# Outputs of one chunk in one run with the next chunk's state products and scores, five shared PSUM banks, and a new order of the first 42 tasks

## The chip, the cores and the metric

The kernel runs on one core of one Trainium2 chip. The metric is device time in microseconds; the median of three runs of the kernel before is 540.75 (540.54 to 540.91). A profile is one execution recorded instruction by instruction, in which PE is TensorE, PEld its weight loads, DVE VectorE, ACT ScalarE, POOL GpSimd and SP the engine that issues most of the transfers.

## The reference

Attention of the RWKV kind goes through 768 steps in 4 batches of 8 heads of 48 channels; its output, 3072 tokens of 384 channels, goes through a feed-forward layer of width 2048.

```python
for t in range(S):
    cur = np.einsum('bhd,bhe->bhde', u[None] * kt, vt)
    y[:, :, t] = np.einsum('bhd,bhde->bhe', rt, state + cur)
    state = wt[:, :, :, None] * state + np.einsum('bhd,bhe->bhde', kt, vt)
...
h = x @ w_in
g = h * (1.0 / (1.0 + np.exp(-1.702 * h)))
return g @ w_out
```

All tensors are float32; r, k, v and w vary per step, u per channel.

## The kernel before, in words

**Attention.** The tokens are cut into 24 chunks of 128 steps, six for each batch. Heads go in four pairs, so rows of a tile are channels (112, with 16 empty ones) and columns are pair and step. `chunk(t)` is a generator; each `next` on it is one piece, token `a<t>` in the order. Its steps: products of the decays from the end and from the start of the chunk (two scans, lines 239 and 245, into `lp`), keys and queries scaled by them (`kq`, 260 and 261), r times k (`rku`, 252), its sum with u (`ps_d`, 267, copied to `s`, 270), keys transposed (`ps_t`, 283, copied to `kt`, 285), the diagonal mask times s (`am`, 292), state updates (`ps_u`, 305) and scores (311) in two banks, the running states `mid` and `sf` (277, 316, 319), scores put over the mask (322), outputs (`ps_y`, 329) and what the states add to them in two halves (340). Between the halves a one-element operation on `mid` that reads the last output bank (349), called the guard here, keeps the second half behind the first. Then the output is split into a high and a low float32r part of `x` (205, 206). From chunk 8 on, s comes from VectorE alone (255, 272, 273).

**Feed-forward.** Four chunks make a group of 512 tokens. A task is one group and one of 16 blocks of the width; the first group's first tasks are cut into halves of 256 tokens, 20 half-width tasks, so there are 106. A task has a first product (token `g`, nine matmuls, 384 to 386, into `ph`), a gelu on ScalarE twice and a subtraction on VectorE (token `h`, 395 to 397, `gh`, `gf`, `gl`), and a second product (token `y`, nine matmuls, 410 to 412, into three banks `po`). Missing rows of `x` are filled by small transfers (token `x`, line 372).

**Weights.** They arrive in twelve pieces (token `f`) and are converted to a high and a low part in four steps each (token `w`, lines 191 to 201) on ScalarE and VectorE, during the first 110 us or so.

**Order.** Each engine does its instructions in the order in which the program issues them. Up to task 42 that order is the list of tokens in `RAMP`; from there `rest()` derives it from `PARTS`, which says for each piece of a chunk at which task before its group's start, and on which side of that task's products, it stands. Token `d` issues dummy matmuls on `warm` (365), `l` loads of a chunk (`wkr_t` in two buffers, on SP and POOL in turn; `v_t` in three), `m` a check of magnitudes on ScalarE (211). PSUM has eight banks: three `po`, two for `ph` and the dummies, three for all attention products.

Of the kernel before, what the change touches and what calls it, by code (L numbers as in the profile page):

```python
# [1 line left out]

# [9 lines left out]
I32 = mybir.dt.int32  # L12
# [35 lines left out]
WHOLE = 8  # L48
LAG = 2
# [15 lines left out]
l0 a0 l0 M a0 a0 d20 l0 l1 m0 a0 f0 a0 a0 d3 a1 a1 a0 a0 d12 a0 m0 a1 a0 a1 a0 l1 f1 a1 a1 d3 w0 l2 a1 m1 a1  # L65
d18 w0 a1 a2 a1 a2 a2 w1 w0 a1 d3 a2 a2 m1 a2 d4 w1 m2 a2 l3 l2 a3 f2 a3 m2 w1 x1 w0 a2 d12 a3 a3 w2 a2 f3 g0
w1 m3 l3 f4 a3 h0 g1 h1 a3 a2 y0 w3 y1 w2 w3 l4 a3 f5 a2 a3 a3 w2 m3 a3 w2 w3 a3 x3 g2 h2 w3 g3 h3 g4 y2 w4 a4
y3 f6 h4 w4 g5 w5 g6 h5 y4 w5 w4 g7 h6 w4 h7 a4 w5 y5 w5 g8 h8 w6 g9 y6 g10 y7 h9 y8 g11 f7 w6 w7 w7 h10 y9
g12 h11 w6 w6 g13 w7 l4 w7 h12 y10 h13 y11 g14 a4 f8 f9 w8 y13 g15 h14 y12 w9 l5 g16 w8 a4 h15 w9 w8 m4 w8 y14
y15 h16 g17 w9 a4 a4 g18 a5 h17 a5 f10 y16 h18 g19 g20 a5 a4 y17 w9 h19 w10 y18 w10 m4 f11 a4 l5 a5 a4 h20 l6  # L70
w11 w10 y19 l7 w11 g21 h21 m5 y20 g22 a5 w10 m5 a6 w11 a5 l6 a4 w11 a4 a5 g23 a6 a5 a5 y21 h22 a6 a6 m6 a5 a6
a7 l8 a5 a7 a6 y22 a6 a7 a6 m6 g24 a7 a6 l7 a7 h23 a7 a6 a6 a7 a7 a7 g25 l9 a7 h24 l8 a7 m7 a8 h25 y23 u a8 a8
x7 m7 y24 y25 l9 g26 m8 a8 h26 g27 h27 g28 a8 a8 y26 a8 y27 a9 a9 h28 g29 l10 y28 a8 g30 a9 m8 h29 a8 m9 g31
h30 a9 a9 l10 a9 a8 a10 a9 a8 y29 g32 y30 h31 y31 a10 a9 h32 l11 a9 g33 g34 l11 m9 a10 m10 h33 y32 g35 m10 a10
a10 a9 h34 a9 a10 l12 g36 a11 a11 y33 h35 a10 g37 a11 h36 y34 m11 h37 a10 a10 g38 a11 a11 g39 m11 a12 a10 l12
a12 a10 a12 a11 a12 a11 a12 y35 h38 y36 a11 l13 a11 a12 h39 g40 a11 m12 l13 a11 x11 y37 l14 m12 a12 y38 g41
y39 h40 a12 a13 h41 l14
# [6 lines left out]
def rwkv_ffn_kernel(ctx: ExitStack, tc, wkr, vp, vrk, ub, w_in, w_out, masks, vt, uc, out):  # L84
# [6 lines left out]
    ps_h = ctx.enter_context(tc.tile_pool(name="ps_h", bufs=2, space=PSUM))  # L91
    ps_a = ctx.enter_context(tc.tile_pool(name="ps_a", bufs=3, space=PSUM))
# [4 lines left out]

    hm = cp.tile([R2, 2 + H], F32, name="hm")
# [36 lines left out]
    warm = at.tile([P, WIDE], BF16, name="warm")  # L135
    V.memset(warm, 1.0)
# [5 lines left out]
    loaded, state, pools = {}, {}, {}  # L142

    def load(t):
# [20 lines left out]
    def fetch(i, pool):  # L165
# [59 lines left out]

    def chunk(t):
# [18 lines left out]
        V.tensor_tensor_scan(  # L245
            pm.rearrange("r p c -> r (p c)"), w0,
            d1f.rearrange("r p c -> r (p c)"), 0.0, op0=ALU.mult, op1=ALU.add,
        )
        s = at.tile([P, H], F32, tag="s", name="s", bufs=2)
        if t < WHOLE:  # L250
            rk = at.tile([R2, NP, C], F32, tag="rku", name="rku")
            V.tensor_tensor(rk, r, k, op=ALU.mult)
# [3 lines left out]
        yield  # L256

        kq = at.tile([R2, 2 * nc_], F32, tag="kq", name="kq", bufs=2)
        kf, qf = (kq[:, i * nc_ : (i + 1) * nc_].rearrange("r (p c) -> r p c", p=NP) for i in range(2))
        V.tensor_tensor(kf, k, li[:, :, 1:CW], op=ALU.mult)  # L260
        V.tensor_tensor(qf, r, pm[:, :, 0:C], op=ALU.mult)
        measures[t] = measured(t, lp, kq)
        yield
        if t < WHOLE:
            ps_d = ps_a.tile([P, NP, 2], F32, tag="psa", name="ps_d")
            for p in range(NP):
                T.matmul(ps_d[:, p], rk[:, p], u_heads[:, p], start=True, stop=True)  # L267
        yield
        if t < WHOLE:
            V.tensor_copy(s, ps_d.rearrange("p n h -> p (n h)"))  # L270
        else:
            V.tensor_tensor(rt, rt, u_sb, op=ALU.mult)
            V.tensor_reduce(s, rt.rearrange("p (h d) -> p h d", d=D), axis=AX.X, op=ALU.add)
        sf = None
        if not first:
            sf = state[t - 1]
            V.tensor_tensor(by_pair(sf), by_pair(sf), total.broadcast_to([R2, NP, D]), op=ALU.mult)
        loaded.pop(t)
        yield
        rows = slice(0, HB if final else P)  # L280
        ps_t = ps_a.tile([P, NP, R2], F32, tag="psa", name="ps_t")
        for p in range(NP):
            T.transpose(ps_t[rows, p], kf[:, p, rows], ident[0:R2, 0:R2])  # L283
        kt = at.tile([P, NP, R2], F32, tag="t", name="kt")
        A.copy(kt[rows], ps_t[rows])
        yield
        am = []
        for h in range(2):
            x_ = at.tile([P, NP, HB], F32, tag=f"am{h}", name="am")
            am.append(x_)  # L290
            for p in range(NP):
                A.activation(x_[:, p], same, AF.Copy, scale=s[:, 2 * p + h : 2 * p + h + 1])  # L292
# [3 lines left out]
        blocks = [slice(HB * b, HB * b + HB) for b in range(2)]  # L296
        both = [ps_a.tile([P, NP * (D + HB)], F32, tag="psa", name=f"ps_u{i}") for i in range(2)]
        us = [x[0:R2, 0 : NP * D].rearrange("r (p d) -> r p d", p=NP) for x in both]
        ps = [x[:, NP * D :].rearrange("r (p c) -> r p c", p=NP) for x in both]
        for p in range(NP):  # L300
            for b, o in enumerate(us[0 : 1 if final else 2]):

# [322 lines left out]
```

## Time and profile before

| what | value |
|---|---|
| median of three runs | 540.75 us |
| the profiled execution | 541.59 us |
| its span, first to last instruction | 539.6 us |
| mean granted clock of TensorE | 0.983 |
| first task starts | 38.30 us |
| last matmul of a task starts | 530.59 us |
| instructions | 11994 |

A row of the timeline is start, duration, engine, line, operation, output<-inputs, tile sizes and count; brackets give the idle time before it and who ended it. Matmuls overlap, so their spacing is read from their starts, and their durations (0.39 us for a big one) are longer than the spacing. A row of waits is who waited, for whom, the sum in us, how often and the longest. A fill or load has a row for its issue on SP, and one that gives the median time to landing.

### The profile page before, as it was taken

Reading aid. Unit: us, or ns where it says so; the run is one execution under the profiler, and the core shown is the slowest. Engines: PE = TensorE matmul, PEld = TensorE weight load, DVE = VectorE, ACT = ScalarE, POOL = GpSimd, SP = SyncE. Lnnn points to the kernel's source line nnn. Section 1 sums busy time; section 2 is a strip of 40 time slices with the busy share of each in tenths; the row PEclk is TensorE's granted clock in tenths of the full one; section 3 lists DMA queues with packets and bytes.
Section 4 is the critical chain, followed back from the end, with each engine's and each line's share of the span. In section 5 each row is a group of like instructions: output and inputs, shape, how many; then the busy total and the mean of one; then the engine's idle time right before and its main releaser. Section 6 shows DMA issues by size and latency. Waiting matters only on the chain.

```text
span 539.6 us, 11994 instructions
## 1 busy us (share of the span) xinstructions
PE 516.1 (96%) x5084; PEld 420.0 (78%) x5089; DVE 283.9 (53%) x515; ACT 276.9 (51%) x644; POOL 27.0 (5%) x68
## 2 busy tenths in 40 slices
PE   6986999999999999999999999999999999999993
PEld 3656999877887777887887877877887887888882
DVE  6797799975655663645545535545545512111110
ACT  2797689856655546455345455445455342422231
POOL 4110110000100001000001000001000001000000
PEclk9997799999999999999999999999999999999998
DMA  8947497123621332333113223113230000100001
GB/s 201 254 118 193 96 290 229 47 62 104 185 78 47 89 91 51 97 117 89 52 38 102 69 96 89 52 38 99 67 102 1 2 1 19 70 0 2 0 1 64
DMA packets 16605, 45.93 MB, mean 85 GB/s; under 512 B 2512, under 2 KB 5904, under 8 KB 16544
## 3 DMA queue, kind: packets, MB, share of 16 engines
q1 hardware_dynamic: 13840, 34.83, 22.2%
q0 software_dynamic: 2592, 9.86, 7.3%
q8 instruction: 42, 0.69, 0.6%
q10 hardware_dynamic: 112, 0.39, 0.2%
q14 instruction: 19, 0.16, 0.1%
HBM read 38.00 MB, written 4.72 MB: 79 GB/s over the span
## 4 chain that ended last, share of the span: by engine, by line
PE 92%; DVE 4%; issue 1%; ACT 1%; DVEq 0%; ACTq 0%
PE po L410 13%; PE ph L384 13%; PE ph L386 13%; PE ph L385 12%; PE po L411 12%; PE po L412 12%; PE ps_y L340 5%; PE ps_y L329 3%; PE ps_u L305 2%; PE ps_u L311 2%; PE ps_t L283 2%; PE ph L365 2%; PE ps_d L267 1%; DVE st L194 1%; DVE lp L245 0%
## 5 line engine op out<-in xcount | busy, mean ns | idle before, releaser
L397 DVE TENSOR_TENSOR gl<-gf,gh 128x512 fp32r<-128x512 f32 (+1 forms) x106 | 67.5, 640 | 190.4 <-ACT gf L396 131.2
L395 ACT ACTIVATE gh<-ph 128x512 fp32r<-128x512 f32 (+1 forms) x106 | 59.0, 557 | 189.5 <-PE ph L386 187.0
L410 PE MATMUL po<-gh,woh 128*128 128x512 f32 (+1 forms) x318 | 122.3, 385 | 0.0
L384 PE MATMUL ph<-x,wih 128*128 128x512 f32 (+1 forms) x318 | 120.7, 380 | 0.0
L386 PE MATMUL ph<-x,wil 128*128 128x512 f32 (+1 forms) x318 | 119.5, 376 | 0.0
L385 PE MATMUL ph<-x,wih 128*128 128x512 f32 (+1 forms) x318 | 119.1, 375 | 0.0
L411 PE MATMUL po<-gh,wol 128*128 128x512 f32 (+1 forms) x318 | 117.9, 371 | 0.0
L412 PE MATMUL po<-gl,woh 128*128 128x512 f32 (+1 forms) x318 | 117.8, 370 | 0.0
L386 PEld LDWEIGHTS ph<-x,wil 128*128 128x128 f32 x318 | 61.1, 192 | 11.0
L384 PEld LDWEIGHTS ph<-x,wih 128*128 128x128 f32 x318 | 61.1, 192 | 10.7
L385 PEld LDWEIGHTS ph<-x,wih 128*128 128x128 f32 x318 | 61.3, 193 | 10.4
L410 PEld LDWEIGHTS po<-gh,woh 128*128 128x128 f32 x318 | 59.9, 188 | 11.1
L412 PEld LDWEIGHTS po<-gl,woh 128*128 128x128 f32 x318 | 59.9, 188 | 10.7
L411 PEld LDWEIGHTS po<-gh,wol 128*128 128x128 f32 x318 | 60.0, 189 | 9.2
L396 ACT ACTIVATE gf<-ph 128x512 f32<-128x512 f32 (+1 forms) x106 | 58.7, 554 | 0.0
L292 ACT ACTIVATE am<-same,s 128x64 f32<-128x64 f32 x192 | 48.7, 354 | 0.1
L340 PE MATMUL ps_y<-kq,mid 48*48 48x64 f32 (+1 forms) x384 | 31.7, 224 | 3.2 <-DVE mid L349 3.2
L340 PEld LDWEIGHTS ps_y<-kq,mid 48*48 48x48 f32 (+1 forms) x384 | 26.1, 131 | 8.7 <-DVE mid L349 4.6
L205 ACT CAST x<-ps_y 112x256 fp32r<-112x256 f32 x48 | 15.8, 382 | 29.4 <-PE ps_y L340 25.5
L239 DVE TENSOR_TENSOR_SCAN lp<-wkr_t,d1r 112x516 f32<-112x516 f32 x24 | 29.4, 1226 | 1.2 <-ACT junk L211 0.6
L245 DVE TENSOR_TENSOR_SCAN lp<-wkr_t,d1f 112x516 f32<-112x516 f32 x24 | 29.4, 1226 | 0.2
L211 ACT ACTIVATE junk<-lp 112x1032 bf16<-112x1032 f32 x24 | 25.6, 1066 | 5.8 <-DVE lp L245 5.8
(73 smaller groups left out, 523.3 us busy)
## 6 DMA issues: line engine op xcount, KB each, us to landing
wkr_t<-in_wkr POOLq DMA_DIRECT2D x12, 577.9 KB, 4.7
wkr_t<-in_wkr SPq DMA_DIRECT2D x11, 577.9 KB, 5.0
st<-in_w_out SPq DMA_DIRECT2D x6, 1024.0 KB, 5.4
rk_t<-in_vrk SPq DMA_DIRECT2D x16, 384.0 KB, 3.7
v_t<-in_vrk SPq DMA_DIRECT2D x24, 192.0 KB, 4.9
st<-in_w_in SPq DMA_DIRECT2D x6, 768.0 KB, 9.2
out_t<-ob SPq DMA_DIRECT2D x18, 256.0 KB, 3.0
st<-in_w_in POOLq DMA_DIRECT2D x12, 128.0 KB, 7.3
```

The costliest lines, as they stand in the source:

```text
L239: V.tensor_tensor_scan(li.rearrange("r p c -> r (p c)")[:, ::-1], w1[:, ::-1], d1r.rearrange("r p c -> r (p c)")[:, ::-1], 0.0, op0=ALU.mu ...
L292: A.activation(x_[:, p], same, AF.Copy, scale=s[:, 2 * p + h : 2 * p + h + 1])
L340: T.matmul(ps[b][head(h), p], from_[head(h), p * D + OFF * h : p * D + HB], qf[head(h), p, blocks[b]], start=False, stop=p == NP - 1, skip ...
L384: T.matmul(ph, h_, xs[i][:, 0, c, cs], start=c == 0, stop=False)
L385: T.matmul(ph, h_, xs[i][:, 1, c, cs], start=False, stop=False)
L386: T.matmul(ph, l_, xs[i][:, 0, c, cs], start=False, stop=c == NM - 1)
L395: A.activation(gh, ph, AF.Gelu_apprx_sigmoid, scale=1.0 / W_SCALE)
L396: A.activation(gf, ph, AF.Gelu_apprx_sigmoid, scale=1.0 / W_SCALE)
L397: V.tensor_tensor(gl, gf, gh.bitcast(F32), op=ALU.subtract)
L410: T.matmul(o, woh[:, f, ms], gh, start=first, stop=False, skip_group_check=True)
L411: T.matmul(o, wol[:, f, ms], gh, start=False, stop=False, skip_group_check=True)
L412: T.matmul(o, woh[:, f, ms], gl, start=False, stop=f == NF - 1, skip_group_check=True)
```

## The change

Of the edits, five matter. `PARTS` gets a rank beside task and side, and three sides instead of two, and the pieces of a chunk are cut anew: the transposes come first in a piece of their own with their copy, the outputs with the first half of the state products stand behind a first product, the next chunk's state updates and scores behind the gelu, and the second half right behind them. All attention and first products draw on one list of five banks, first in, first out; dummies are put ahead of whatever takes the next bank. ScalarE copies `s` and, for the first eight chunks, does the guard; from chunk 8 on VectorE multiplies the masks. `kq` is one instruction instead of two, `sf` has three buffers instead of two, `gf` one instead of two. Loads that alternated between SP and POOL all go on SP. `RAMP` is a new list.

```diff
+BANKS = 5
+BY_ACT = range(WHOLE)
-PARTS = [("a", 0, 0), ("a", 1, 0), ("a", 2, 0), ("m", 2, 0), ("a", 2, 1), ("a", 3, 0), ("m", 3, 0), ("l", 3, 0),
-         ("l", 3, 0), ("a", 3, 1), ("a", 4, 0), ("a", 4, 1), ("a", 5, 1), ("a", 6, 1), ("a", 7, 1), ("x", 7, 1)]
+PARTS = [("a", -2, 2, 7), ("a", -1, 1, 7), ("a", 0, 1, 6), ("a", 1, 0, 5), ("m", 0, 2, 4), ("a", 1, 1, 4),
+         ("a", 1, 1, 7), ("a", 1, 2, 0), ("a", 1, 2, 3), ("a", 1, 2, 7), ("m", 1, 2, 7), ("a", 2, 1, 1),
+         ("l", 3, 0, 2), ("l", 6, 1, 0), ("a", 5, 1, 7), ("a", 5, 2, 7), ("a", 6, 0, 1), ("x", 6, 2, 0)]
...
-    ps_h = ctx.enter_context(tc.tile_pool(name="ps_h", bufs=2, space=PSUM))
-    ps_a = ctx.enter_context(tc.tile_pool(name="ps_a", bufs=3, space=PSUM))
+    ps_a = ctx.enter_context(tc.tile_pool(name="ps_a", bufs=1, space=PSUM))
...
-            (nc.sync, G)[t % 2].dma_start(a[ROWS], wkr[t])
+            nc.sync.dma_start(a[ROWS], wkr[t])
...
+    def bank(name):
+
+        i = free.pop(0)
+        x = ps_a.tile([P, WIDE], F32, tag=f"bank{i}", name=name)
+        held[id(x)] = i, x
+        while cold:
+            for _ in range(cold.pop()):
+                T.matmul(x.rearrange("p (n c) -> p n c", c=P), warm, warm_b, start=True, stop=True)
+        return x
+
+    def release(*xs):
+
+        for x in xs:
+            free.append(held.pop(id(x))[0])
...
-        V.tensor_tensor(kf, k, li[:, :, 1:CW], op=ALU.mult)
-        V.tensor_tensor(qf, r, pm[:, :, 0:C], op=ALU.mult)
+        V.tensor_tensor(kq, kr, scale, op=ALU.mult)
...
-            V.tensor_copy(s, ps_d.rearrange("p n h -> p (n h)"))
+            A.copy(s, got[:, 0:H])
+            release(got)
...
+            if t in BY_ACT:
+                for p in range(NP):
+                    A.activation(am[h][:, p], same, AF.Copy, scale=s[:, 2 * p + h : 2 * p + h + 1])
+            else:
+                s_h = s.rearrange("p (n h) -> p n h", h=2)[:, :, h : h + 1]
+                V.tensor_tensor(am[h], same_b, s_h.broadcast_to([P, NP, HB]), op=ALU.mult)
...
-        V.copy_predicated(mid[0:1, OFF : OFF + 1], never, ps[1][0:1, NP - 1, HB - 1 : HB])
+        (A.copy if t in BY_ACT else V.tensor_copy)(mid[0:1, 0:1], ps[1][0:1, NP - 1, HB - 1 : HB])
         yield
         inter(((1, 0), (0, 1)))
...
-        gf = mo.tile([P, WIDE], F32, tag="gf", name="gf")[:, 0:n]
+        gf = mo.tile([P, WIDE], F32, tag="gf", name="gf", bufs=1)[:, 0:n]
...
+        release(got)
         V.tensor_tensor(gl, gf, gh.bitcast(F32), op=ALU.subtract)
```

TensorE in the steady part, one chunk, before. Names: `po_...` second products, `ph` first products, `ps_y` outputs, `ps_t` transposes, `ps_u` state updates and scores.

```order
L329 MATMUL ps_y_3338<-am,v_t_87 48x64
...
L340 MATMUL ps_y_3338<-kq,sf_89 64x64
...
L410 MATMUL po_2987<-gh,woh 128x512
...
L386 MATMUL ph<-x,wil 128x512
L340 MATMUL ps_y_3339<-kq,mid_90 64x64
...
L283 MATMUL ps_t<-ident,kq 128x112 x4
L410 MATMUL po_2987<-gh,woh 128x512
```

The same place in the changed kernel:

```order
L280 MATMUL ps_t<-ident,kq 128x112 x4
L404 MATMUL ph<-x,wih 128x512
...
L352 MATMUL ps_y_3429<-am,v_t_84 48x64
...
L363 MATMUL ps_y_3429<-kq,sf_89 64x64
...
L323 MATMUL ps_u_3466<-v_t_85,kt 64x48
...
L329 MATMUL ps_u_3466<-kq 64x64
...
L363 MATMUL ps_y_3430<-kq,mid_91 64x64
...
L431 MATMUL po_2953<-gh,woh 128x512
```

Before, a task's products stand between the two halves of the state products, and the state updates (line 305) come two products later in a run of their own; after, both halves, the state updates and the scores are one run, and the transposes are alone between two products.

VectorE at the start, from the first scan on, before:

```order
L239 SCALAR_TENSOR_TENSOR lp<-wkr_t_83,d1r 112x516
L243 RECIPROCAL d1f<-lp 112x4
L245 SCALAR_TENSOR_TENSOR lp<-wkr_t_83,d1f 112x516
L252 TENSOR_TENSOR rku<-wkr_t_83 112x512
L260 TENSOR_TENSOR kq<-wkr_t_83,lp 112x512
L261 TENSOR_TENSOR kq<-wkr_t_83,lp 112x512
L270 COPY s<-ps_d 128x8
L239 SCALAR_TENSOR_TENSOR lp<-wkr_t_84,d1r 112x516
```

And in the changed kernel:

```order
L262 SCALAR_TENSOR_TENSOR lp<-wkr_t_82,d1r 112x516
L265 RECIPROCAL d1f<-lp 112x4
L267 SCALAR_TENSOR_TENSOR lp<-wkr_t_82,d1f 112x516
L273 TENSOR_TENSOR kq<-wkr_t_82,lp 112x1024
L288 TENSOR_TENSOR rku<-wkr_t_82 112x512
L262 SCALAR_TENSOR_TENSOR lp<-wkr_t_83,d1r 112x516
```

The copy of `s`, which reads TensorE's `ps_d`, no longer stands between the first and the second chunk's scans, and `kq` comes ahead of `rku` in one instruction.

More of the change, by code (lines that the diff above doesn't have):

```diff
@@ L1 @@
 from contextlib import ExitStack
+from dataclasses import replace
 import concourse.bass as bass
@@ L95, in rwkv_ffn_kernel @@
     at = fast.enter_context(tc.tile_pool(name="at", bufs=1))
+    warm = at.tile([P, P], BF16, name="warm")
+    V.memset(warm, 1.0)
     hm = cp.tile([R2, 2 + H], F32, name="hm")
@@ L140, in rwkv_ffn_kernel @@
     G.memset(acc, 0.0)
-    loaded, state, pools = {}, {}, {}
+    loaded, state, pools, cold, held, free = {}, {}, {}, [], {}, list(range(BANKS))
     def load(t):
@@ L244, in chunk @@
         yield
[L245 to L248, printed above, removed]
+        V.tensor_tensor_scan(pm, w0, d1f.rearrange("r p c -> r (p c)"), 0.0, op0=ALU.mult, op1=ALU.add)
+        yield
+        kq = at.tile([R2, 2, NP, C], F32, tag="kq", name="kq", bufs=2)
+        kf, qf = kq[:, 0], kq[:, 1]
+        scale = lp[:, 1 : n + 1]
+        scale = replace(scale, ap=[list(scale.ap[0]), [n - 1, 2], [CW, NP], [1, C]])
+        V.tensor_tensor(kq, kr, scale, op=ALU.mult)
+        measures[t] = measured(t, lp, kq.rearrange("r i p c -> r (i p c)"))
+        yield
+        rows = slice(0, HB if final else P)
+        got = bank("ps_t")
+        ps_t = by_p(got, R2)
+        for p in range(NP):
+            T.transpose(ps_t[rows, p], kf[:, p, rows], ident[0:R2, 0:R2])
+        kt = at.tile([P, NP, R2], F32, tag="t", name="kt")
+        A.copy(kt[rows], ps_t[rows])
+        release(got)
+        yield
         s = at.tile([P, H], F32, tag="s", name="s", bufs=2)
@@ L255, in chunk @@
             V.tensor_tensor(rt, rt, kt_, op=ALU.mult)
[L256 to L262 removed]
+            V.tensor_tensor(rt, rt, u_sb, op=ALU.mult)
+            V.tensor_reduce(s, rt.rearrange("p (h d) -> p h d", d=D), axis=AX.X, op=ALU.add)
+        loaded.pop(t)
         yield
         if t < WHOLE:
[L265 removed]
+            got = bank("ps_d")
+            ps_d = by_p(got, 2)
             for p in range(NP):
@@ L269, in chunk @@
         if t < WHOLE:
[L270 to L278, printed above, removed]
-        yield
[L280 to L292, printed above, removed]
-        yield
[L296 to L299, printed above, removed]
+            A.copy(s, got[:, 0:H])
+            release(got)
+        am = [at.tile([P, NP, HB], F32, tag=f"am{h}", name="am", bufs=2) for h in range(2)]
+        for h in range(2):
+            if t in BY_ACT:
+                for p in range(NP):
+                    A.activation(am[h][:, p], same, AF.Copy, scale=s[:, 2 * p + h : 2 * p + h + 1])
+            else:
+                s_h = s.rearrange("p (n h) -> p n h", h=2)[:, :, h : h + 1]
+                V.tensor_tensor(am[h], same_b, s_h.broadcast_to([P, NP, HB]), op=ALU.mult)
+        yield
+        both = [bank(f"ps_u{i}") for i in range(2)]
+        us = [by_p(x[0:R2], D) for x in both]
+        ps = [by_p(x[:, NP * D :], HB) for x in both]
         for p in range(NP):
@@ L311, in chunk @@
                     T.matmul(ps[h][b, p], kf[head(h), p, b], qf[head(h), p, b], start=True, stop=True)
-        mid = mids[t % 2]
+        yield
+        sf, mid = None if first else state[t - 1], mids[t % 2]
         if first:
@@ L322, in chunk @@
             V.copy_predicated(am[h], after_b, ps[h])
+            release(both[h])
         yield
-        ps = [ps_a.tile([R2, NP, HB], F32, tag="psa", name=f"ps_y{b}") for b in range(2)]
+        got = [bank(f"ps_y{b}") for b in range(2)]
+        ps = [by_p(x, HB) for x in got]
         for p in range(NP):
@@ L356, in chunk @@
             cs = slice(col * C + b * HB, col * C + b * HB + HB)
-            split(x[0:R2, 0, :, cs], x[0:R2, 1, :, cs], ps[b])
-        state.pop(t - 1, None)
+            split(x[0:R2, 0, :, cs], x[0:R2, 1, :, cs], ps[b][0:R2])
+            release(got[b])
         yield
-    def keep_warm(n):
-        ph = ps_h.tile([P, WIDE], F32, tag="ph", name="ph")
-        for _ in range(n):
-            T.matmul(ph, warm[:, 0:P], warm, start=True, stop=True)
     def fill_x(x, c0, c1):
@@ L380, in first_product @@
         cs = slice(c0 * C, c1 * C)
-        ph = ps_h.tile([P, WIDE], F32, tag="ph", name="ph")[:, 0 : (c1 - c0) * C]
+        got = bank("ph")
+        ph = got[:, 0 : (c1 - c0) * C]
         for c in range(NM):
@@ L462, in do @@
             elif kind == "d":
-                keep_warm(i)
+                cold.append(i)
             elif kind == "u":
@@ L513, in rwkv_ffn_kernel @@
     V.tensor_reduce(oks, acc, axis=AX.X, op=ALU.add)
-    ps = ps_a.tile([1, 1], F32, tag="psa", name="ps_n")
+    ps = bank("ps_n")[0:1, 0:1]
     T.matmul(ps, oks, oks, start=True, stop=True)
```

99 lines of the change are left out of this document (53 added, 46 removed).

## The prediction

> **What bounds the kernel now.** I read the page's busy times first, then a table of stretches. In it the columns are the stretch, its length, busy time and count of PE, PEld, DVE, ACT and POOL, the granted clock and the DMA share.
>
> ```profile
> PE 516.1 (96%) x5084; PEld 420.0 (78%) x5089; DVE 283.9 (53%) x515; ACT 276.9 (51%) x644; POOL 27.0 (5%) x68
> 38.30:63.13 24.83, 20.44 (x279) 19.33 (x279) 17.14 (x32) 16.32 (x38) 2.50 (x5) 0.73 0.64 174
> 63.13:139.99 76.86, 75.61 (x918) 68.79 (x916) 66.59 (x108) 60.20 (x135) 5.08 (x10) 1.00 0.48 138
> 139.99:530.98 390.99, 389.72 (x3475) 313.39 (x3473) 169.96 (x327) 175.80 (x418) 9.80 (x19) 1.00 0.21 59
> ```
>
> From 140 us on TensorE is busy 389.7 of 391.0 us while VectorE and ScalarE are under half: there only less work on TensorE, or cheaper switching between kinds of it, can save time. Before that it is a ramp. TensorE starts its first feed-forward task at 38.30, and up to 63.13 it lacks work (20.44 of 24.83) and runs at a mean clock of 0.73. Here VectorE, ScalarE and the chain of the first four chunks decide. So the change is costed in two places.
>
> **Term A: fewer switches of the array.** One steady chunk before, on TensorE (start, duration, instruction):
>
> ```profile
> 265.68 0.39 PE L386 MATMUL ph<-x,wil 128*128 128x512 f32 x1
> 266.00 0.69 PE L329 MATMUL ps_y<-am,v_t 64*48 64x64 f32 x32
> 267.08 0.50 PE L410 MATMUL po<-gh,woh 128*128 128x512 f32 x1
> ...
> 269.25 0.39 PE L384 MATMUL ph<-x,wih 128*128 128x512 f32 x1
> ...
> 271.07 0.39 PE L386 MATMUL ph<-x,wil 128*128 128x512 f32 x1
> 271.39 0.27 PE L340 MATMUL ps_y<-kq,mid 64*64 64x64 f32 x1
> ...
> 271.99 0.60 PE L283 MATMUL ps_t<-ident,kq 112*128 112x112 f32 x4
> ...
> 274.50 0.39 PE L384 MATMUL ph<-x,wih 128*128 128x512 f32 x1
> ...
> 276.31 0.39 PE L386 MATMUL ph<-x,wil 128*128 128x512 f32 x1
> 276.63 0.62 PE L305 MATMUL ps_u<-v_t,kt 64*64 64x48 f32 x30
> 277.72 0.50 PE L410 MATMUL po<-gh,woh 128*128 128x512 f32 x1
> ...
> 279.89 0.39 PE L384 MATMUL ph<-x,wih 128*128 128x512 f32 x1
> ```
>
> Big matmuls follow each other every 0.227 us (274.50 to 276.31 holds eight of them: 1.81/8). A run of small ones costs the time between the big matmuls around it, less that spacing. From 265.68 to 269.25 are 3.57 us with ten spacings (2.27): outputs with their first state products cost 1.30. The second state products with the transposes cost 274.50 - 271.07 - 2.27 = 1.16. State updates with scores cost 279.89 - 276.31 - 2.27 = 1.31. Together 3.77 us a chunk, in three runs.
>
> How much of it is switching? State updates and scores take 277.72 - 276.63 = 1.09 to the next big matmul; of this I count some 0.14 as the way out (an estimate, from how long the 64-row runs above stand beyond their last starts), so 0.95 is work, and 1.31 - 0.95 = 0.36 is what entering and leaving costs. The second state products hold 271.99 - 271.39 = 0.60, less the same 0.14: 0.46. In the merged run (outputs, first products, state updates, scores, second products) the switching is paid once: 1.30 + 0.95 + 0.46 = 2.71. The transposes then stand alone. Such a place exists before:
>
> ```profile
> 146.05 0.39 PE L386 MATMUL ph<-x,wil 128*128 128x512 f32 x1
> 146.28 0.55 PE L283 MATMUL ps_t<-ident,kq 112*128 112x112 f32 x4
> ...
> 148.76 0.39 PE L410 MATMUL po<-gh,woh 128*128 128x512 f32 x1
> ```
>
> 148.76 - 146.05 - 2.27 = 0.44 us: they take 0.31 to the next matmul, so they are nearly free to enter and leave. New sum per chunk 2.71 + 0.44 = 3.15, a saving of 0.62. The order has eleven such merged runs in the steady part (6.8 us); the last chunk goes from two runs to one (0.36); and in the ramp, after the first two tasks, the runs that leave the full array go from 18 to 14 (1.4). **A = -8.6 us.** Lower end: if every run, the lone transposes too, pays 0.36, only the count of runs matters, 56 to 42, so -5.0. Upper end -9.5, if the merged run's inner seams are free too (0.08 less each).
>
> The Trainium skill, page TensorEngine Tiling (Array Packing), section Tiling Modes, says that a switch of the tiling mode drains TensorE, while a mere change of tile does not. By it the transposes, on the full array, pay nothing, and A is near its upper end; counting all runs alike would give the lower end. The 0.44 row agrees with the rule.
>
> **Cover of the merged run.** Between first and second state products stands a one-element copy that reads the last output bank and holds back the second half. Its price when nothing covers it:
>
> ```profile
> PE ps_y L340 <- DVE mid L349: 2.5, 8, 0.3
> PE ps_y L329 <- DVE am L322: 2.0, 2, 1.7
> L397 DVE TENSOR_TENSOR gl<-gf,gh 128x512 fp32r<-128x512 f32 x86 | 59.4, 690 | 187.2 <-ACT gf L396 128.0 <-PE ps_t L283 29.7 <-PE ps_u L311 29.4
> L285 ACT COPY kt<-ps_t 128x448 f32<-128x448 f32 x20 | 11.0, 550 | 12.0 <-PE ps_t L283 11.9
> wkr_t<-in_wkr SPq DMA_DIRECT2D x11, 577.9 KB, 5.0
> ```
>
> The first two rows are waits; the next two groups with their mean in ns; the last a load with its time to landing. The guard's wait is 0.3 us of idle TensorE, eight times after 60 us; with the last matmul's own 0.22 us about half a microsecond. The merged run puts 0.95 us in its place, and on VectorE the instructions ahead of the copy (the three on r and k) are due many microseconds earlier, so it is hidden; with a 0.69 us gelu subtraction in front it would show by some 0.4 to 0.6. Six bare cases remain instead of eight: **-0.6 us**. The state updates need the transposed keys, which ScalarE copies in 0.55 us behind the lone transposes; a whole first product (2.04 us) and the outputs lie between. Masks move from ScalarE (eight instructions) to VectorE (two) for the chunks from 8 on, where VectorE is busy 170 of 391 us: nothing. SP takes over the odd loads of POOL, behind its own stores and fills; a load lands in 5.0 us and is issued three tasks ahead of its scan (3 x 18 x 0.227 = 12 us), so I cost that at nothing while the queue is not held for 7 us.
>
> **Term B: the ramp.** VectorE decides when the fourth chunk's x is split, which with its fill lets task 5 start.
>
> ```profile
> 5.27:56.85 51.58, 43.97 (x656) 31.25 (x660) 40.78 (x71) 34.83 (x81) 5.25 (x10) 0.90 0.72 185
> DVE mid L349 <- PE ps_y L340: 3.3, 3, 2.2
> DVE s L270 <- PE ps_d L267: 2.4, 1, 2.4
> DVE mid L316 <- PE ps_u L311: 2.3, 2, 1.2
> DVE x L206 <- ACT x L205: 1.9, 2, 1.5
> 40.92 1.22 DVE L201 TENSOR_TENSOR wol<-c,woh 128x1024 fp32r<-128x1024 f32 x1
> 42.05 0.16 DVE L270 COPY s<-ps_d 128x8 f32<-128x8 f32 x1
> 42.13 0.35 DVE L277 TENSOR_TENSOR sf<-sf,lp 112x192 f32<-112x192 f32 x1
> 42.39 0.76 DVE L397 TENSOR_TENSOR gl<-gf,gh 128x256 fp32r<-128x256 f32 x2
> ...
> 43.84 0.21 DVE L349 COPY_PREDICATED_SCALAR mid<-after,ps_y 1x1 f32 x1 [0.69 <-PE ps_y L340]
> 43.98 1.20 DVE L194 SCALAR_TENSOR_TENSOR st<-st 128x1024 int32<-128x1024 int32 x1
> ...
> 46.35 1.22 DVE L194 SCALAR_TENSOR_TENSOR st<-st 128x1024 int32<-128x1024 int32 x1
> ```
>
> Between the first scan (5.27) and the end of that split (56.85) VectorE works 40.78 us and idles 10.8. Ahead of the same split the changed order drops four copies of s (0.08 each from start to start) and four guards (0.14), both now ScalarE's, and adds one pair on staged weights (43.98 to 46.35, 2.37), one low part (1.13) and two gelu subtractions (0.38 each): +3.4, so 44.2 us. Of the idle time the waits of s (2.4) and of the guard (3.3) leave with their instructions; 5.1 stay. The split then ends at 5.27 + 44.2 + 5.1 = 54.6.
>
> ```profile
> 31.35 2.04 SPq L372 DMA_DIRECT2D x<-x  x3
> x<-x SPq DMA_DIRECT2D x6, 32.0 KB, 2.3
> 63.01 0.28 PE L412 MATMUL po<-gl,woh 128*128 128x256 f32 x1
> 63.13 0.28 PE L384 MATMUL ph<-x,wih 128*128 128x256 f32 x1
> ```
>
> The fill's three issues take 2.04 and land 2.3 later, so task 5 can start at 58.9 against 63.13 before. Before, TensorE itself was late there: tasks 2 to 4 came behind the whole fourth chunk, at half clock; in the new order 2 to 4 and two second products stand ahead of that chunk and fill its wait. And one more second product (nine of 0.12, 1.1 us) is done by then. **B = -(63.13 - 58.9) - 1.1 = -5.3 us.** With all 10.8 us of idle kept it is +0.4, with none -10.4; the middle lies near the rows that name the waits. From there to the second group VectorE has 66.6 us of work in 76.9, so a lead on both engines is kept, not eaten.
>
> **New waits in the ramp.** Chunks 4 to 7 come closer together between tasks 22 and 26, and banks are shared. One run that holds a chunk's scores and its outputs waited 1.7 us for the masks (the am row above). I take **+1.5**, between 0 and 5. The 24 dummy matmuls less (75 to 51) all stand ahead of the first task, in time that TensorE waits anyway.
>
> **Sum.** -8.6 - 0.6 - 5.3 + 1.5 = -13.0. The profiled execution took 541.59 us, 1.99 more than its span of 539.6, and the median of the runs is 540.75, 0.84 below it. 539.6 - 13.0 = 526.6 of span, 528.6 in a profiled run, **527.7 us as a median**; its own range is 521 to 533 from the ends of A, B and the new waits.
>
> **Rivals.**
> The ramp gains nothing: waits for shared banks, or a clock that falls again. For it: the clock was 0.73 over 38.30 to 63.13 after gaps of one to two microseconds, and a gap stays in the fourth chunk's run. Then only A, -0.6 and +1.5 remain: 540.75 - 7.7 = 533. Against it: tasks now stand where the gap was. The Trainium skill, page TensorE: Matmul & The Clock Gate, section Part 1, has the clock halve after an idle window of some 3.4 us; here it halved after shorter gaps, so the measurement counts.
>
> The guard is not covered in the merged run: eleven times 0.6 us, 527.7 + 6.6 = 534.
>
> Slower: gf has one buffer instead of two, so ScalarE's second gelu of a task waits until VectorE has subtracted the task before, and everything behind it in ScalarE's queue waits too. Place: the 20 half-width tasks, where VectorE and ScalarE are both nearly full. If each meets half of a weight pair (1.2 us), that is 24 us, 552 us in all; it decides from 13.0/20 = 0.65 a task. Against it: the subtractions are spread between the weight pieces one by one, as the gelus are.
>
> That the change does not do what it says is excluded by the order; that its parts cancel within 0.2% stays possible.
>
> **Chances.** Forecast 0.68; ramp gains nothing 0.14; guard uncovered 0.07; gf slower 0.08; cancelled 0.03. A measurement of this kernel tells 0.2% (1.1 us) from no change. Faster 0.89, same 0.03, slower 0.08. The range 521 to 534 holds the forecast and the two middle rivals, and leaves out the slow one and the far ends.
>
> **What would show it.** A: lone transposes near 0.44 us, merged runs near 2.7, four tasks with a chunk in 19.5 us instead of 20.1. Guard: no wait before the second state products past 150 us. B: the fourth chunk's x split near 54.6 and task 5 near 59, with the clock back at 1.00 there. Wrong would be: ScalarE waiting for gl in the half-width tasks, TensorE waiting for a bank (a first product behind gelu or x), or the first task later than 38.

## The result, and the profile after

The changed kernel takes **526.15 us** (median; 525.13 to 527.66) against 540.8 for the kernel before: a ratio of 0.973, 95% interval 0.9705 to 0.9759. Thirteen timings of it in all, with the later ones, give 524.05 to 529.40 and a median of 526.16; that is the value the experiments are compared with. The profiled execution is the slowest of the first four (527.66, span 525.9).

The page's busy times of the kernel after, and its table of stretches (columns as before), cut where the first task, task 5 and task 26 start and a microsecond ahead of the last product:

```profile
PE 503.6 (96%) x5065; PEld 417.0 (79%) x5065; DVE 295.7 (56%) x507; ACT 250.6 (48%) x532; POOL 13.7 (3%) x45
33.33:58.00 24.67, 20.96 (x294) 19.92 (x295) 21.73 (x36) 19.43 (x44) 1.49 (x3) 0.79 0.88 244
58.00:137.56 79.56, 77.01 (x977) 70.09 (x975) 64.67 (x96) 60.70 (x143) 1.50 (x3) 0.98 0.43 118
137.56:517.30 379.74, 378.46 (x3406) 310.96 (x3402) 181.26 (x338) 144.95 (x285) 5.98 (x12) 1.00 0.20 59
```

TensorE is busy 12.5 us less, and each stretch begins earlier: task 5 at 58.00 instead of 63.13, task 26 at 137.56 instead of 139.99. But the middle stretch got longer, 79.56 instead of 76.86 us, and its clock is no longer 1.00. One steady chunk on TensorE:

```profile
258.14 0.50 PE L431 MATMUL po<-gh,woh 128*128 128x512 f32 x1
...
272.33 0.39 PE L433 MATMUL po<-gl,woh 128*128 128x512 f32 x1
272.57 0.55 PE L280 MATMUL ps_t<-ident,kq 112*128 112x112 f32 x4
...
274.78 0.39 PE L406 MATMUL ph<-x,wil 128*128 128x512 f32 x1
275.10 0.69 PE L352 MATMUL ps_y<-am,v_t 64*48 64x64 f32 x32
...
277.58 0.50 PE L431 MATMUL po<-gh,woh 128*128 128x512 f32 x1
...
279.75 0.39 PE L404 MATMUL ph<-x,wih 128*128 128x512 f32 x1
```

By the prediction's measure (time between the big products around a run, less nine or ten spacings of 0.227 us) the lone transposes cost 274.78 - 272.33 - 2.04 = 0.41 us and the merged run 279.75 - 274.78 - 2.27 = 2.70. Four tasks and a chunk take 277.58 - 258.14 = 19.44 us instead of 20.11. The ramp: end of the fourth chunk's x split on VectorE, the fill behind it with its median time to landing, and TensorE's step to task 5.

```profile
54.40 0.75 DVE L209 TENSOR_TENSOR x<-ps_y,x 112x256 fp32r<-112x256 f32 x2
x<-x SPq DMA_DIRECT2D x3, 32.0 KB, 2.1
57.89 0.28 PE L433 MATMUL po<-gl,woh 128*128 128x256 f32 x1
58.00 0.28 PE L404 MATMUL ph<-x,wih 128*128 128x256 f32 x1
```

TensorE's clock was 0.50 from 48 to 57 us in this profile, and full again at task 5. TensorE's largest waits over the whole span after (the last two are the guard's), and ScalarE's for `gl`:

```profile
PE ps_y L352 <- DVE am L342: 2.7, 2, 1.7
PE ps_t L280 <- DVE kq L273: 2.5, 2, 1.8
PE ps_y L363 <- issue: 2.3, 1, 2.3
PE ps_u L323 <- ACT s L303: 1.5, 1, 1.5
PE ph L404 <- ACT junk L214: 1.3, 1, 1.3
PE ps_y L363 <- DVE mid L372: 1.3, 5, 0.3
PE ps_y L363 <- ACT mid L372: 1.3, 5, 0.3
ACT gf L416 <- DVE gl L418: 2.5, 6, 1.0
```

I had not foreseen the third row. Its place in TensorE's timeline, and the stretches that follow:

```profile
122.48 0.38 PE L363 MATMUL ps_y<-kq,mid 48*48 48x64 f32 x4
125.15 0.37 PE L363 MATMUL ps_y<-kq,mid 48*48 48x64 f32 x3 [2.29 <-issue]
125.45 0.80 PE L431 MATMUL po<-gh,woh 128*128 128x512 f32 x1
...
129.30 0.50 PE L363 MATMUL ps_y<-kq,mid 64*64 64x64 f32 x5
```

```profile
126.00:127.00 1.00, 1.00 (x4) 0.77 (x3) 0.19 (x1) 0.00 (x0) 0.00 (x0) 0.50 0.40 155
127.00:128.00 1.00, 1.00 (x4) 0.81 (x3) 0.00 (x0) 0.00 (x0) 0.00 (x0) 0.50 0.01 3
129.00:130.00 1.00, 1.00 (x31) 0.70 (x33) 0.00 (x0) 0.00 (x0) 0.00 (x0) 1.00 0.00 0
```

In the middle of a row of equal small products TensorE stands for 2.29 us, and the profile names nothing that it waits for (`issue`). Behind it the clock is halved, and the nine big products take 129.30 - 125.45 = 3.85 us instead of 2.04. Together 4.1 us.

### The profile page after: what moved, and what is told of

It reads as the page before. It is cut to its first block, busy times and chain, and to the rows that moved or that the text cites. A ratio compares the mean times of both kernels' runs of the same rounds, so it can differ in the third digit from the quotient of the medians.

```text
span 525.9 us, 11810 instructions
## 1 busy us (share of the span) xinstructions
PE 503.6 (96%) x5065; PEld 417.0 (79%) x5065; DVE 295.7 (56%) x507; ACT 250.6 (48%) x532; POOL 13.7 (3%) x45
## 4 chain that ended last, share of the span: by engine, by line
PE 89%; DMA 5%; DVE 3%; ACT 1%; issue 1%; SPq 0%; DVEq 0%; ACTq 0%
PE po L431 13%; PE po L432 13%; PE ph L404 13%; PE po L433 13%; PE ph L406 12%; PE ph L405 12%; PE ps_y L363 4%; DMA wkr_t<-in_wkr 3%; PE ps_y L352 3%; PE ps_u L329 2%; PE ps_u L323 2%; DMA st<-in_w_in 2%; PE ps_t L280 1%; PE ps_d L300 1%; DVE lp L262 0%
## 5 line engine op out<-in xcount | busy, mean ns | idle before, releaser
L432 PE MATMUL po<-gh,wol 128*128 128x512 f32 (+1 forms) x318 | 119.5, 376 | 0.0
L406 PE MATMUL ph<-x,wil 128*128 128x512 f32 (+1 forms) x318 | 118.3, 372 | 0.0
L431 PEld LDWEIGHTS po<-gh,woh 128*128 128x128 f32 x318 | 61.2, 193 | 11.6
L433 PEld LDWEIGHTS po<-gl,woh 128*128 128x128 f32 x318 | 61.3, 193 | 10.6
L404 PEld LDWEIGHTS ph<-x,wih 128*128 128x128 f32 x318 | 59.9, 188 | 12.4 <-ACT junk L214 1.8
L432 PEld LDWEIGHTS po<-gh,wol 128*128 128x128 f32 x318 | 61.3, 193 | 10.1
L406 PEld LDWEIGHTS ph<-x,wil 128*128 128x128 f32 x318 | 59.9, 188 | 11.4 <-issue 0.3
L405 PEld LDWEIGHTS ph<-x,wih 128*128 128x128 f32 x318 | 60.0, 189 | 10.1
L273 DVE TENSOR_TENSOR kq<-wkr_t,lp 112x1024 f32<-112x1024 f32 x24 | 29.3, 1221 | 6.1 <-PE ps_y L363 5.7
L363 PE MATMUL ps_y<-kq,sf 64*64 64x64 f32 (+1 forms) x320 | 25.9, 223 | 0.0
```

Source lines behind the costliest of these rows:

```text
L363: T.matmul(ps[b][head(h), p], from_[head(h), p * D + OFF * h : p * D + HB], qf[head(h), p, blocks[b]], start=False, stop=p == NP - 1, skip ...
L404: T.matmul(ph, h_, xs[i][:, 0, c, cs], start=c == 0, stop=False)
L405: T.matmul(ph, h_, xs[i][:, 1, c, cs], start=False, stop=False)
L406: T.matmul(ph, l_, xs[i][:, 0, c, cs], start=False, stop=c == NM - 1)
L431: T.matmul(o, woh[:, f, ms], gh, start=first, stop=False, skip_group_check=True)
L432: T.matmul(o, wol[:, f, ms], gh, start=False, stop=False, skip_group_check=True)
```

## The experiments

**The kernel again.** The edit is none; the question was whether the stall is part of the kernel.

> The changed kernel once more. Theory (TensorE's wait of 2.3 us inside a group of four matmuls near 123 us comes from the loads in flight there, in which the fetch of its own instructions is late): the wait is there again at the same instruction, 0.5 to 3 us, and the median is 525 to 527. Rival (a chance event of that one execution): no such wait, and the span some 3 to 4 us shorter than 525.9.

525.97 us; the stall is there again, at the same product (123.94, 1.80 us), this time with the clock at 1.00 behind it. It recurs, 1.66 to 2.62 us long, in every kernel below but three: the one with late loads, the one with the stream moved, and the one with 22 cold products, whose loads are late too.

**One run more per chunk.**

```diff
-("a", 5, 2, 7), ("a", 6, 0, 1)
+("a", 6, 0, 0), ("a", 6, 0, 1)
```

The second half of the state products goes one task's outputs later, into a run of its own.

> The second half of the state products stands one second product later than in the changed kernel, as a run of its own, in the eleven steady chunks; all else stays. Theory (each excursion from the full array costs 0.36 us): slower by 11 x 0.36 = 4.0 us, 529 to 531. Rival (the gain came from the ramp, excursions are hidden): within 1 us of the changed kernel.

529.49 us (ratio 0.9805, 0.9779 to 0.983), 3.3 more than the changed kernel. In the profiles, the time from the start of task 26 to that of the last product, which holds all eleven runs, is 384.80 instead of 380.83 us: 4.0 more. TensorE's timeline:

```profile
273.03 0.39 PE L406 MATMUL ph<-x,wil 128*128 128x512 f32 x1
...
277.31 0.39 PE L433 MATMUL po<-gl,woh 128*128 128x512 f32 x1
277.64 0.31 PE L363 MATMUL ps_y<-kq,sf 48*48 48x64 f32 x2
...
280.19 0.39 PE L406 MATMUL ph<-x,wil 128*128 128x512 f32 x1
```

The first run costs 277.31 - 273.03 - 2.04 = 2.24, the second 280.19 - 277.31 - 2.04 = 0.84: 3.08 for what takes 2.70 in one run. The same products cost 0.38 us more for one more way out of the full array and back, eleven times: 4.2. The prediction's 0.36 per run is confirmed by an edit that moves these products and nothing else. The Trainium skill, page TensorEngine Tiling (Array Packing), section Tiling Modes, says that a switch of the tiling mode drains TensorE; this trace agrees and gives the price, 0.38 us for both ways.

**The transposes inside the run.**

```diff
-("a", 1, 0, 5)
+("a", 1, 1, 3)
```

> The transposes move from between two products to the head of the merged run, eleven times. Theory of the tiling mode (a lone run of transposes stays on the full array and pays 0.1 us at most): 0 to 1.2 us faster. Rival (every run pays 0.36, whatever it holds): faster by 11 x 0.36 = 4 us. If the copy of the transposed keys is then late for the state updates, a wait on ACT kt shows and it is slower.

527.32 us (0.9746, 0.972 to 0.9772): no gain; the 1.2 us more are within the intervals. From task 26 to the last product it is 380.65 us, against 380.83. The timeline:

```profile
274.97 0.39 PE L406 MATMUL ph<-x,wil 128*128 128x512 f32 x1
275.20 0.55 PE L280 MATMUL ps_t<-ident,kq 112*128 112x112 f32 x4
275.68 0.69 PE L352 MATMUL ps_y<-am,v_t 64*48 64x64 f32 x32
...
280.10 0.39 PE L433 MATMUL po<-gl,woh 128*128 128x512 f32 x1
```

280.10 - 274.97 - 2.04 = 3.09 with the transposes in, 2.70 + 0.41 = 3.11 with them alone. Standing alone costs them nothing, so what the lower bound of term A stands on (all runs pay alike) is refuted.

**The guard without cover.**

```diff
-("a", 5, 2, 7)
+("a", 5, 2, 2)
```

The second state products come directly behind the first, ahead of the state updates and scores.

> The second half of the state products comes right behind the first, ahead of state updates and scores, so that nothing covers the guard in the eleven steady chunks; the runs stay as many. Theory (the merged run hides a round trip of about half a microsecond): slower by 11 x 0.3 to 0.6 = 3.3 to 6.6 us, and a wait on the guard's line in each. Rival (the guard costs nothing): within 1 us.

532.31 us (0.9865, 0.9831 to 0.9898), 6.2 more. The wait from 160 us on, in the changed kernel and then in this one, and the run's frame on TensorE:

```profile
PE ps_y L363 <- DVE mid L372: 1.0, 4, 0.3
PE ps_y L363 <- DVE mid L372: 3.8, 15, 0.3
```

```profile
272.32 0.39 PE L406 MATMUL ph<-x,wil 128*128 128x512 f32 x1
...
274.04 0.27 PE L363 MATMUL ps_y<-kq,mid 64*64 64x64 f32 x1 [0.26 <-DVE mid L372]
...
277.52 0.39 PE L433 MATMUL po<-gl,woh 128*128 128x512 f32 x1
```

277.52 - 272.32 - 2.04 = 3.16 instead of 2.70. The eleven waits more are those of the eleven steady chunks. An uncovered guard costs 0.46 us, of which 0.26 show as waiting; eleven times is 5.1, and from task 26 to the last product it is 386.31 us, 5.5 more. The rest of the 6.2 was not found in the profile, which is of this kernel's fastest execution (529.11).

**The tasks behind the fourth chunk.**

```diff
-... y0 h1 w3 g2 a3 a3 y1 g3 a2 f4 f5 g4 w4 m3 ... w4 h2 f7 w3
-w3 a3 y2 h3 a3 ...
+... y0 h1 w3 a3 a3 y1 a2 f4 f5 w4 m3 ... w4 f7 w3
+w3 a3 g2 h2 g3 g4 y2 h3 a3 ...
```

> In the ramp the first products of the third to fifth task (g2, g3, g4), which the changed order puts between the pieces of the fourth chunk, go behind that chunk's kv products, where the kernel before had them; everything else as changed. Theory (step B of the prediction: the start of the products is what the new sequence gains): the work that the three tasks' products filled is idle again, so the same TensorE work ends later. The three products are 8.2 us at full clock and cover waits of the fourth chunk; expected 3 to 6 us slower than the changed kernel, that is 529 to 532 us, with waits of TensorE of over 3 us more before 62 us and, if the clock halves in them, task 5 at 61 to 64 us instead of 58.0. Rival (step B was worth nothing, the ramp is bounded by the chain of loads and VectorE): within 1 us of the changed kernel, 525 to 527 us.

530.09 us (0.979, 0.9762 to 0.9818), 3.9 more, inside the expected 3 to 6. The x split starts at 57.12 instead of 54.40 and task 5 at 60.80 instead of 58.00, just under the expected 61 to 64. The clock is 0.50 to 0.56 from 42 to 56 us; in the changed kernel it is at 0.50 from 48 to 57 only. What the longer half clock alone costs was not tried. My expectation also took the three products at 8.2 us; they are 27 matmuls of half width, and at 0.12 us each 3.2 us at full clock.

**The copy of s on VectorE.**

```diff
-            A.copy(s, got[:, 0:H])
+            V.tensor_copy(s, got[:, 0:H])
```

> One line: the copy of the scores out of the bank goes back from ScalarE to VectorE, as in the kernel before; everything else as changed. Theory (the ramp's x split of the fourth chunk waits for VectorE, so each copy taken from it brings that split forward): 16 copies of some 0.25 us on VectorE, 4 of them in the ramp, the split ends up to 1 us later and TensorE waits again for VectorE before state products; expected 0.5 to 2.5 us slower than the changed kernel, 526.5 to 528.5 us. Rival (the engine of this copy is not on the path that sets the end, neither in the ramp nor behind it): within 0.5 us, 525.5 to 526.5 us; the waits for the copy (1.5 us on ScalarE before a state product in the ramp) may even go down.

531.33 us (0.9814, 0.9793 to 0.9836): 5.2 more, twice the expected upper end. VectorE in the first 60 us, as a wait and as an instruction:

```profile
DVE s L303 <- PE ps_d L300: 3.3, 2, 2.2
```

```profile
18.27 0.17 DVE L303 COPY s<-ps_d 128x8 f32<-128x8 f32 x1 [2.16 <-PE ps_d L300]
18.35 0.77 DVE L342 COPY_PREDICATED am<-after,ps_u 128x256 f32<-128x256 int32 x2
```

The copy is short; what costs is that VectorE stands behind it until TensorE has made `ps_d`, and everything queued there stands too. The first task starts at 35.51 instead of 33.33 (32.10 in the second profile of the changed kernel), the x split at 57.11 instead of 54.40, task 5 at 60.60 instead of 58.00. How the rest of the 5.2 us comes about was not followed. My expectation priced the copies and not the wait, though the profile of before had that wait (2.4 us).

**Where does the stall come from?** No DMA and no semaphore releases the stalled product, but instructions come by DMA too. The page lists an instruction queue (packets, MB, share of the DMA engines):

```profile
q8 instruction: 42, 0.69, 0.5%
```

That these 42 packets of 16 KB are TensorE's is read from their number: it executes 5,065 products and 5,065 weight loads, some 240 to a packet. The DMA engines were full when the stall began (a share of 1.01 from 122 to 123 us), so the first suspects were the loads. Two kernels move them and nothing else, one of them a load step later,

```diff
-... l8 l9 l8 g25 ... a7 a6 l9 y23 a6 ... a7 a7 x7 h25
+... l8 l9 l8 g25 ... a7 a6 y23 a6 ... a7 a7 x7 l9 h25
```

and, with the loads apart,

```diff
-... l8 l9 l8 g25 ... a7 a6 l9 y23 a6 ... a7 a7 x7 h25
+... l8 l8 g25 ... a7 a6 l9 y23 a6 ... a7 a7 x7 l9 h25
```

> In the ramp the last two transfers of the tenth chunk's loads (its v and rk, issued at 122.7 us in the changed kernel) are issued some 10 us later, behind the fetch of x; no instruction of TensorE, VectorE or ScalarE moves. Theory (TensorE stops inside a run of small products at 122.9 us, 1.7 to 2.6 us in each profile so far, because its instructions come late while the loads of two chunks fill the DMA engines): if these last two transfers are what delays it, the stall and the half clock that follows it in some executions are gone, 2 to 4 us faster than the changed kernel, 522 to 524 us. Rival 1 (the transfers issued up to 120.2 us suffice, 1.15 MB that are still in flight at 122.9): the stall stays, and the time too, 525 to 527 us. Rival 2 (the place in the instruction stream decides, not the loads): the same, stall and time stay.

> As in loads_spread, and the tenth chunk's wkr, 0.58 MB, is issued behind the ninth's v and rk instead of ahead of them, after the run of small products in which TensorE stops; again no instruction of TensorE, VectorE or ScalarE moves. Only the ninth chunk's v and rk, 0.58 MB, are then issued between 118 and 122 us, and at the 240 to 400 GB/s of that window they have landed before the stalling product. Theory (transfers in flight delay TensorE's instructions): no stall at that product, full clock behind it, 2 to 4 us faster than the changed kernel, 522 to 524 us, and less spread from run to run. Rival 1 (place in the instruction stream): stall and time stay, 525 to 527 us. Rival 2 (the stall goes elsewhere: the loads now collide with a later run of small products): a wait of TensorE on nothing of over 1 us later than 130 us, time 524 to 527 us.

526.56 (0.9733, 0.9718 to 0.9748) and 526.71 us (0.9749, 0.9731 to 0.9767): no gain, and the stall stays, 2.49 and 2.26 us. With the loads apart, the stretches around it:

```profile
122.00:123.00 1.00, 0.94 (x55) 0.79 (x46) 0.57 (x2) 1.00 (x6) 0.00 (x0) 1.00 0.37 90
123.00:124.00 1.00, 0.00 (x0) 0.00 (x0) 1.00 (x2) 1.00 (x3) 0.00 (x0) 1.00 0.00 0
124.00:125.00 1.00, 0.00 (x0) 0.00 (x0) 0.97 (x4) 0.47 (x2) 0.00 (x0) 1.00 0.00 0
```

TensorE stands for two microseconds while the DMA engines do nothing. As I had stated it, the theory falls: a load in flight does not hold the stalled products. But one of the loads (wkr) was still issued at 119.18, against what my expectation said, and TensorE's instruction packet began only at 122.56, when that load was nearly through. So two more kernels: one with all three loads of the tenth chunk behind the fetch of x, one that leaves the loads and moves the instruction stream by 102 places.

```diff
-... l8 l9 l8 g25 ... a7 a6 l9 y23 a6 ... a7 a7 x7 h25
+... l8 l8 g25 ... a7 a6 y23 a6 ... a7 a7 x7 l9 l9 h25
```

```diff
-                T.matmul(x.rearrange("p (n c) -> p n c", c=P), warm, warm_b, start=True, stop=True)
+                for q in range(2):
+                    half = x.rearrange("p (n c) -> p n c", c=P)[:, 2 * q : 2 * q + 2]
+                    T.matmul(half, warm, warm_b[:, 0:2], start=True, stop=True)
```

> All three transfers of the tenth chunk's loads (1.15 MB, issued at 118.9 to 123.1 us in the changed kernel) are issued behind the fetch of x, after 131 us; no instruction of TensorE, VectorE or ScalarE moves. In the run before this one (the same with one of them, wkr, still issued at 119.2 us) the stall stayed, 2.26 us, though the DMA engines were idle (share 0.00) in its last two microseconds; but TensorE's own instruction packet of 16 KB had come only at 122.5 us, when that transfer was through. Theory L (the packet is held up by the transfers): with nothing issued between 115 and 131 us the packet comes some microseconds earlier, before 119 us, and the stall and the half clock are gone: 2 to 4 us faster than the changed kernel, 522 to 524.5 us. Rival P (the place in the instruction stream alone, 256 instructions per packet and a run of some 230 that lasts 2.2 us): packet within the run, stall and time stay, 525 to 527 us.

> Each of the 51 cold products of the ramp, which only keep the clock up and whose results nobody reads, is cut into two of half the columns: the same columns, 51 products and 51 weight loads more, so every later TensorE instruction stands 102 places further on in the stream, all of it before 31 us. Loads as in the changed kernel. Theory P (the stall comes where the end of a packet's 256 instructions falls late into the run of small products, its 202nd instruction, so that the packet behind it had to come while 200 instructions went by in 2 us): the end of that packet now falls 102 instructions earlier in the run, and it was asked for over 10 us ahead; the stall is gone at this place: 2 to 4 us faster, 522 to 524.5 us. Theory L (the transfers alone decide, wherever the ends of packets fall): a stall of over 1 us at another place of the same run, time as changed, 525 to 527 us. Both may be true together: then this one and the one with late loads are both faster.

524.62 us (0.9701, 0.9683 to 0.9718) and 524.34 us (0.9696, 0.9677 to 0.9714), and the stall is gone in both. With late loads the same products run through at full clock:

```profile
121.36 0.23 PE L352 MATMUL ps_y<-am,v_t 64*64 64x64 f32 x2
121.42 0.55 PE L363 MATMUL ps_y<-kq,mid 48*48 48x64 f32 x7
121.90 0.50 PE L431 MATMUL po<-gh,woh 128*128 128x512 f32 x1
```

The start of the packet, found in the queue's records in steps of 0.1 us, tells these two kernels from the rest:

| kernel | packet begins | run of small products begins | TensorE goes on |
|---|---|---|---|
| changed | 122.27 | 121.03 | 125.15, after 2.29 us |
| changed, second profile | 121.29 | 120.31 | 123.94, after 1.80 |
| one load step later | 121.19 | 119.74 | 124.06, after 2.49 |
| loads apart | 122.56 | 121.11 | 125.20, after 2.26 |
| late loads | 119.16 | 119.97 | no stall |
| stream moved | 115.64 and 124.79 | 121.68 | no stall |

With the stall, the packet begins 1.0 to 1.5 us into the run, and TensorE goes on 2.6 to 2.9 us after that begin. Without the loads it begins 0.8 us ahead of the run; with the stream moved none begins in it.

The place in the stream can be counted. Of all TensorE's recorded instructions (products, weight loads and those of its sequencer), the stalled product at 123 us is number 3010, in two of the ten profiles 3009. The two later stalls, with the stream moved and with 22 cold products, are at numbers 706 and 2754: nine times 256 and once 256 ahead of 3010. So TensorE stops at the border between two packets, of 256 instructions each. With late loads the packet begins when TensorE is at number 2795, 215 ahead of that border; in the ten profiles with the stall it begins at 2935 to 3009, at most 75 ahead. At this place both are needed: a border in a run of small products (here 104 of them with their weight loads, 208 instructions in 2 us), and loads behind which the next packet begins late. How the loads hold the packet back the runs do not show. Moving the stream makes a new meeting of the two at another place, in the ramp:

```profile
PE ps_d L302 <- issue: 1.1, 1, 1.1
```

There TensorE goes on at 28.16, 2.8 us after a packet that begins at 25.36, with the DMA engines full. So the same 2.5 to 2.9 us were met at a place that nobody had picked.

**The measure again, and the first pause.** The last two kernels are the changed one once more and the one with late loads and four cold products more.

```diff
-m0 m0 d18 a0
+m0 m0 d22 a0
```

> The changed kernel as it is, in five rounds, as the measure for the kernel with late loads. Theory (the stall of 1.7 to 2.6 us at 123 us is in every execution, and the half clock behind it in those where it lasts longest): 525 to 528 us, above the 523.3 to 525.4 us of the kernel with late loads, and the stall in the profile. Rival (that difference was chance): a median at or below 525 us.

> The kernel with late loads, with 22 instead of 18 cold products ahead of the first chunk's transposes. TensorE's first wait, for the first scaled keys at 9.4 us, was 1.72 to 2.89 us in the profiles so far; where it was 2.29 or more, the clock was halved for some 3 us behind it, where it was 1.84 or less it was not. Four products of 0.37 us more bring it to 0.2 to 1.4 us. Theory 1 (a pause of more than about 2.27 us halves the clock): full clock from 9 to 20 us in the profile. Theory 2, on the time: TensorE waits again and again for VectorE and for loads up to 32 us, so the half clock costs nothing there: 524 to 525 us, as with 18. Rival: it is the source of the spread from run to run, and the time goes to 522 to 523.5 us with a spread under 1 us.

The changed kernel: 526.16 us (0.9719, 0.9699 to 0.9738), stall of 2.29. Its interval overlaps those of late loads and of the moved stream; but all ten timings of these two kernels (523.14 to 525.38) are below the median of the thirteen with the stall, and the medians differ by 1.5 to 1.8 us. The kernel with 22 cold products: 525.33 us (0.9715, 0.9702 to 0.9728). Its first pause and its stall (in the row of the stretch TensorE's busy time, the clock and the DMA engines):

```profile
1.14 6.37 PE L238 MATMUL ps_t<-warm 128*128 128x512 bf16 x22 [1.14 <-DVE warm L101]
9.45 0.57 PE L280 MATMUL ps_t<-ident,kq 112*128 112x112 f32 x4 [1.94 <-DVE kq L273]
```

```profile
9.00:12.00 3.00, 2.55 (x52) 0.82 1.03 224
117.39 0.51 PE L405 MATMUL ph<-x,wih 128*128 128x512 f32 x1 [1.11 <-issue]
```

I expected a pause of 0.2 to 1.4 us at full clock, from 0.37 us for each product; the 22 took 0.29 us each and were over at 7.51, where 18 had been over at 6.58 with late loads and at 7.77 in the second profile of the changed kernel. The pause was 1.94, and the clock behind it 0.82. So a limit of 2.27 us is not what decides whether the clock is halved here. As the pause was not shortened as meant, whether it makes the spread between runs was not tested. The eight instructions more also brought a new stall, 1.11 us, 2.9 us after a packet at 114.49. In time, the 0.7 us more than late loads are within the intervals.

## Why the prediction was right, and where it was not

Predicted 527.7 us, range 521 to 534; measured 526.15. Point by point, in the first profile after:

- **Term A** was right, and the steady part agrees nearly to the digit. The run cost 2.70 (predicted 2.71), the transposes 0.41 (0.44), four tasks and a chunk 19.44 (19.5). From task 26 to the last product it is 518.39 - 137.56 = 380.83 us after (the last product's start) and 530.59 - 139.99 = 390.60 before: 9.8 less. Of that, 1.7 us are work that the new order has done before task 26 (a chunk's transposes, state updates and scores, 0.41 + 1.31). The 8.1 left stand against 7.8 of the prediction (eleven runs, the last chunk and the guard).
- **The guard** was right: from 200 us on no wait stands ahead of the second state products in the eleven merged runs, and of eight bare waits past 60 us six are left, as forecast, at 0.26 us instead of 0.3 (five on VectorE's copy, one on ScalarE's). Uncovered it costs 0.46 us each (predicted 0.6), in all 5.5 us of the steady part and 6.2 of the medians (predicted 6.6).
- **Term B** had the right path and two sizes off, which partly cancel. The x split ends at 55.15 (54.6), half a microsecond late; task 5 starts at 58.00 (58.9), with the clock just back at full. The sum let it wait for the last of the fill's three issues to land, 2.04 + 2.3 = 4.3 us behind the split; it began 2.9 us behind it. The first piece lands 2.1 us after its issue, and TensorE steps from a second product straight into task 5 without a wait. With the second product more that is done, the lead is 5.1 + 1.1 = 6.2 us against 5.3. Two of its causes were tried alone: tasks ahead of the fourth chunk are worth 3.9 us, the copy of `s` off VectorE 5.2. Their sum is more than the lead, so they are not separate parts of it.
- **New waits in the ramp**, +1.5, is the step whose cause failed. I looked for shared banks and masks. No product waits for a bank: the 1.5 us that the row of waits puts down to the copy of `s` end 0.05 us behind the copy of `kt`, which that product reads, and the 1.3 us ahead of the first task end with its fill. The two waits for masks (2.7 us in all) end at 23 and 49 us, ahead of this stretch. What came in their place is the instruction packet: 2.29 us, and 1.8 of half clock where it follows. Between task 5 and task 26 the lead shrank from 6.2 to 2.4 + 1.7 = 4.1 us, 2.1 lost, where the prediction had about nothing (1.5 of waits, 1.4 of saved runs). Without the 4.1 us of this stall the stretch would have gained 2.0. The two kernels without it bear this out: with late loads the stretch takes 75.73 us, with the stream moved 75.45, that is 3.8 and 4.1 less than 79.56.
- **The end.** From the last product's start to the end of the span are 525.9 - 518.39 = 7.5 us after, 539.6 - 530.59 = 9.0 before. These 1.5 us were in no term, and what makes them was not tried.
- **Median against profile**: I carried over 0.84 us; the profiled execution after lies 1.5 above the median. The kernel after varies more (5 us instead of 1), and only part of that is the stall: without it 2.2 us remain.

Added up on the span: -6.2 + 2.1 - 8.1 - 1.5 = -13.7, and 539.6 - 525.9 is 13.7. The forecast's -13.0 was close partly by luck: a cost that I had not known and gains that I had not counted cancel.

Of the rivals, "the ramp gains nothing" is refuted by the lead of 6.2 us, though the clock did fall again there (0.50 from 48 to 57 us); "guard uncovered" by the waits and by its own run, and "gf slower" by 2.5 us of ScalarE waiting for `gl` in the whole span, where it needed 13. Two buffers for `gf` were not tried.

## What to carry to other kernels

Count how often the small products leave the full array, not only how many there are: 0.38 us for each time here, while transposes on the full array may stand where they like. A copy that reads another engine's result belongs on the engine whose queue can stand still; price the wait, not the copy. And a long run of short instructions needs its code as well as its data: keep large loads out of the microseconds ahead of it, or look where its packets end, here every 256 instructions.

## What the hardware showed that was not expected

- TensorE stands still for want of instructions. Each such stall of over a microsecond in the profiles of the runs above stood at a border of 256 instructions and ended 2.5 to 2.9 us after the begin of a 16 KB packet in the instruction queue; the twelve lasted 1.1 to 2.6 us, and at 123 us the product was always the same. Late loads alone removed it, and so did 102 instructions ahead of it.
- A half clock after short pauses. Of the ten stalls at 123 us, the five up to 2.26 us (1.66, 1.73, 1.80, 2.26, 2.26) were followed by full clock, the five from 2.29 us on (2.29, 2.29, 2.49, 2.59, 2.62) by 0.50 to 0.67 over four microseconds. The Trainium skill, page TensorE: Matmul & The Clock Gate, section Part 1, has an idle window of some 3.4 us; here less was enough. No fixed length holds either: at the first pause of the ramp 2.11 us left the clock at 1.00 and 1.94 us took it to 0.82. What else decides stays open.
